# A chunked delta rule with an MLP on one core: K·Q^T and K·state as one product, and a new order of all steps

## The chip, the cores and the metric

The kernel runs on one core of one Trainium2 chip. The metric is the device time of one execution in microseconds (us). A core has a matrix engine (TensorE, PE in the profile, with its weight loads shown as PEld), a vector engine (VectorE, DVE), an activation engine (ScalarE, ACT), a general engine (GpSimd, POOL), and queues that start DMA transfers, most of them on SyncE (SP). Each engine works through its own instructions in order; engines wait for each other by semaphores. All data is 32-bit float.

## The reference

Two blocks stand one behind the other. The first is the delta rule, for 4 batches and 8 heads (32 heads), 768 tokens and 48 channels a head; the state of a head is a 48x48 matrix:

```python
k_n = k / (np.linalg.norm(k, axis=-1, keepdims=True) + 1e-06)
for t in range(S):
    y[:, :, t] = q_t @ state
    v_old = k_t @ state
    state = state + b_t * outer(k_t, v_t - v_old)
```

Its output, 384 channels a token, is x of the second block, an MLP with a residual:

```python
xn = (x - mu) / np.sqrt(var + 1e-06) * g_ln
out = x + np.maximum(xn @ w_ch1, 0.0) @ w_ch2      # 384 -> 1536 -> 384
```

## The kernel before, in words

The tokens are cut into 12 chunks of 64. The 32 heads lie in 16 columns of tiles, and in two halves of the 128 partitions; a product of one chunk for all heads is 64 small matmuls, four of them at a time in the four quadrants of TensorE's array. In the loop `for j ... for hp, e in hp_e`, `hp` picks the half of the partitions the operands are read from, and `e` the half that the result is written to.

Per chunk `c` the recurrence is written in matrices: G is K times K^T, from which VectorE computes a triangular inverse for the two halves of a chunk, row by row (`rows_inverse`, lines 910 and 917, for two chunks at once); `join` (lines 984 and 990) completes it with two small products. Then, in this order of dependence:

- `queries`: P = K times Q^T (line 822, into the PSUM tile `two`, 64 columns a head), and one VectorE instruction that multiplies it with a triangular mask into the tile `pt` (line 853). P does not need the state, so it may be made ahead.
- `recur`: `ks` = K times the state (line 1036 into `two`, 48 columns), which VectorE subtracts from v (line 1043); `qs` = Q times the state (line 1036 into `by`), which starts the sum of the output; `u` = inverse times v (line 1091 into `two`, copied to `u` by ScalarE, line 1093); `s` = K^T times u (line 1108), which VectorE adds to the state `s_all` (line 1118); `y` = P times u (line 1098), added to `qs` in `by` and copied to x by ScalarE (line 1136).
- LayerNorm of x (lines 1142 to 1154), a transposition, from chunk 3 on with a round trip through DRAM, and the MLP of that chunk. From chunk 3 on the first MLP product is computed with 15 block products per chunk (line 1311, sums on the other engines), the second with 7 (line 1527); chunks 1 and 2 use plain products for the first (line 1430), chunk 0 for both (lines 1410 and 1452).

Nothing but data links the MLP of one chunk with the recurrence of later chunks, so the steps of both are mixed. Every step (an engine, a function that issues its instructions, the keys that it reads and writes) is given to `Line.add`. The mixed order is written out by hand in the string `ORDER`: numbers of steps, and the letter `f` for a filler, a product of zeros with 256 columns (line 1605) that keeps TensorE busy. `emit` issues the steps in that order, and `in_this_order` pins the order on every engine, so a step that waits holds up all that stand behind it on its engine. The numbers in `cost`, `due` and `cap` belong to the planner that wrote the order and change nothing at run time.

`two` and `by` are two PSUM tiles of two banks each. G of later chunks, P, `ks`, `u` and `s` use `two`; `qs`, `y` and, from chunk 6 on, `join` use `by`. The MLP uses four other banks.

Of the kernel before, what the change touches and what calls it, by code (L numbers as in the profile page):

```python
# [16 lines left out]
C = 64  # L17
# [114 lines left out]
57 52 54 58-59 56 65-66 10-13 25 14 0 22 28 43 8 44 9 5 7 53 55 79 6 71 77 72 89 37 96 76 97 90 1-2 86 85 80 88 98  # L132
91 105 92 99 15 26-27 23 16 34-35 29-30 17 36 100 93 101 31 19 94 87 103 82 81 104 84 24 83 18 95 102 20-21 118 32
124 74 73 106-107 78 69 38 119 108 219-220 75 39 109 120 33 125 110-111 70 40 f 130-131 126 112 122 128 121 123 f f
f 132 134 400 113 405 64 63 262 257-258 313 411 256 260-261 263 404 410 259 311 68 322 312 403 310 399 324 323 325
67 409 402 408 398 133 136 135 41 45 62 254 225 129 127 231 137 f 140 145 213 138 211 235 139 144 142 141 f f f 146
143 241 245 f f 148 253 47 46 42 659 49-51 147 150 154-155 153 149 156 661 60-61 246 152 157 151 4 f f f 162-163 236
115 114 242 217 243 159 221 160 227 212 161 223 247 264 663 255 48 222 166-168 158 265-266 170-171 169 f f 164 f f
178 215 116 412 229 117 237 224 165 267-268 179 172 182 206-207 270 269 232 184 271-272 183 174 173 664 248 660 208
273 3 274-275 209 226 238 177 175-176 185 210 186-187 f f f 180 314 316 315 194 317 240 244 214 276 181 188 239  # L140
192-193 191 195 277-278 189 279 198 318-319 201 199-200 190 280-281 216 282 228 283 f 196-197 284 334 326 361 367
320 285-288 335 289-292 202 327 338 366 360 293-299 203-204 233 340 342-343 300 328-329 346 205 f f f f 330-331
347-348 671 218 397 230 396 234 352 336-337 339 353 332 354-355 572 574 673 665 662 341 251 249 573 344 575 358-359
250 345 349-350 576 578 406 362 577 579 301 407 321 333 432 431 309 307 302-303 308 304 473 306 305 471-472 474 788
351 356 363 357 252 658 415 433-434 582 580 598 370 364 581 599 373 435 604 583 605 368 584 610 586 365 413 470 414
611 585 588 416 372 587 475 590 401 787 790 792 789 791 793-794 589 379 417 591 378 592-596 616 600 374 597 602 601
606 418 376 603 608 436 666 369 476-479 481-489 480 490-495 375 496-499 670 675 672 1073 674 677 377 371 676 500
419-420 501 617 607 380 635 609 636 614 391 421 437 502-507 381 508 795 509 439 510-519 424 615 423 612 620 438 384
390 382 425 422 426 429-430 428 427 637 621 440-441 638 385 392 442 639 445 394 386 447 443 520-523 444 524 393
525-527 622-623 667 624 640 383 678 387 668 446 388 613 389 679-680 528 450 529 395 1085 625-626 618 530 451 448 455  # L150
531 456 449 452 532 650 533 457 534 453-454 535-536 651 537 641 627 642-643 628-629 644 796 458 462 645 630 538 652
539-544 653 631 464 460 465 619 646 461 463 459 826 921 1181 784 928 785 925 669 929 681 924 922 684 686 683 685 545
682 786 687 827 797 647 632 798-799 688-691 694 832 830-831 833 828 838 829 693 1087 1075 1077 1074 695-696 654
697-701 634 930 549 547-548 546 633 931-932 702-706 800 707-709 656 710 550 834 839 844-845 836 933 649 934-935 850
1079 1078 1089 1086 1076 853 851-852 466-467 837 551 859 842 835 552-555 1072 1084 556 860-861 840 862 557-558 560
559 711-713 655 714-715 692 716 561 717-728 562 801 863 841 846 802 864 805 854 856 866 927 843 857 855 936 729 565
564 563 566 865 803 807 806 730 810 808 848-849 809 811 815 812 847 731 804 876-877 869-870 732 813 871 937 567 872
814 733 816 734 817 735-736 822 818 886-887 878 820 825 568 823 819 570-571 569 821 824 468 867 858 469 1090 868 883
938-939 873 888-889 874 737 1080 738 941 890-891 940 942 1179 1176 1184 648 1178 1186 923 926 1177 1366 1188 1185
1187 1183 739-740 657 741 875 742-746 879 747-751 892 943 752-757 1365 1190 1189 880 894 881 895-896 944 901-902 897  # L160
903 898-899 946 945 1547 1088 1091 900 882 1092 1096 893 885 884 1081-1082 1191 975 1182 1558 1371 904 977 1093 905
947 978 1094 948 951 761 760 1083 1095 759 758 1097 1100 1373 1098-1099 983 912 906-907 913-915 984 989 916-917 1192
918 990 920 1370 1372 1375 1652 1377 1369 1376 1378 1180 1368 1379 1374 909 919 979 981 995 949-950 953-954 952 956
762 1193 763 1194-1195 982 765 996 980 985 1101 764 767 766 986 1559 972 908 910-911 1001 1004 969 1548 970 976 971
955 957 959 958 1102 1561 1549 1196 1103-1105 1107-1109 1002 1551 1550 1563 1110-1121 987 991 1010-1012 768 988 992
772 993 1003 1007 1122 1013-1015 769 994 770-771 999 1197 1000 1016 1020-1022 997 1027-1028 998 1198 1023-1024
773-775 777 1201 1199 1123 1560 1005-1006 1017 1008 1018 1565 1564 1553 1546 1552 1124-1125 960 974 1126-1135 1009
1019 1224 1034 1562 1136 1037-1040 1025 961 1654 1380 1137 1026 1200 973 1138 1029-1030 1035 1041-1042 1045
1031-1032 962-963 965 1367 964 1655 1658 1660 1662 1844 1664 1845 1139 1046 1381 1047-1048 1033 1043 1554 1049-1050
1052-1053 1225 1044 1228-1229 1226 968 967 778 966 1243 1232 1036 1051 1202 776 1203 1054-1055 1063 779 783 781-782  # L170
780 1056 1064-1065 1057 1066 1140 1382 1384 1383 1141 1204 1206 1142 1207 1205 1143 1058 1144 1244-1245 1233 1236
1234 1067 1237 1068 1239 1230 1247 1145 1385 1211 1235 1208 1146 1212 1147 1238 1209 1069 1248 1386-1387 1249
1240-1241 1227 1251 1266 1252 1059 1250 1242 1148-1149 1213 1210 1150 1214-1215 1388 1267 1231 1651 1070 1659 1846
1661 1275 1060 1246 1389 1216 1566 1151 1263-1264 1253 1256 1260-1261 1254 1262 1152-1153 1280 2047 1285 2035 1555
1257 1556 1271 1255 1154 1265 1268 1276 1269 1272 1155 1258 1156-1158 1270 1159 1273 1567 1277 1286 1281 1287
1160-1161 1259 1568 1278 1162-1164 1288 1165 1279 1289 1274 1166-1170 1062 1071 1657 1663 1219 1217 1220 1218 1557
1061 1222-1223 1221 1569 1650 1171 1573 1282 1390 1290 1303 1313 1291-1292 1314 1293 1304-1307 1315-1318 1308 1665
1309 1850 1574 1572 1571 1849 2141 1174-1175 1173 1653 1172 1294-1295 1297 1413 1296 1298 1301 1300 1299 1319
1283-1284 1666 1320 1310 1338 1330 1339 1420 1311 1302 2037 1312 1667 1106 1575 1321 1656 1327 1322-1323 1340
1331-1335 1341 1324-1325 1414-1415 1576-1577 1336 1345 1342-1343 1326 1417 1346 1328-1329 2036 1337 1570 1347 1418  # L180
1348-1350 1578-1579 1582 1351 1344 1679 1356 1391-1392 1424 1581 1352 1583-1584 1432 2039 1428 1456 2049 1421 1357
1416 1358-1361 1422 1429 1433 1585 1393 1586 1668 1587 1419 1588 1362 1589-1591 1395 1592-1593 1669 1430 1434
1425-1426 2038 1435 1353 1466 1447-1448 1461 2046 2051 1671 1423 1431 1670 1673 1672 1427 1594 1436 1444 1437 1445
1441-1442 1449 1595 1681 1596 1443 1450 1674 1452 1597 1396 1394 1451 1397 1400 1598-1599 1446 1600 1453 1462 1457
1438 1458 1676-1678 1675 1401 1454 1601 1455 1398 1602 1467-1468 1463 1603 1399 1604 1439 1605 1459 1606 1460 1680
1402 1607 1469 1682 1608 1494-1495 1484 1496 1471 1485 1472 1486-1487 1440 1470 1683 1488-1489 1684 1686 1475-1476
1478 1477 1490 1482 1403 1609-1610 1404 1473 1611 1464-1465 1474 2048 2040 1481 1479-1480 1852 1842-1843 1612 1860
1613 1501-1503 1497-1498 1504 1499 1354 1854 1851 1853 1855 1847 1364 1355 1363 2139 1856 2138 2143 1405 1857 1685
1492 1491 1483 1493 1858 1511 1505-1506 1614 1407 2145 1409 2146 2142 1408 1406 2148 2150 2147 2152 2149 1500 1512
1519 1615 1859 1616-1617 1513 1520 1514-1516 1618 1517 1521 2050 2041 1508 1518 1848 2034 1510 1522-1523 1526 1524  # L190
1527-1528 1525 1507 1529-1531 1688 1410 1687 1412 1709 1411 1619 1720 1509 1716 2052 1620 1689 1691 1532 1692
1696-1697 1690 1693 1621-1625 1698 2042 1694 1537 1871 1861 1713 1865 1862 1864 1863 1538 1710-1712 1539-1540 1714
# [1560 lines left out]
```

## Time and profile before

| what | value |
|---|---|
| three timed runs | 516.07, 517.01, 518.98 us (median 517.01) |
| profiled execution, first to last instruction | 514.1 us; no other time of it is given |
| TensorE busy | 493.1 us (96%) |
| VectorE busy | 353.5 us (69%) |
| GpSimd busy | 284.8 us (55%) |
| ScalarE busy | 206.9 us (40%) |
| P of chunk: line 822, `two`, from qt and kt, 64 matmuls in a chunk | 1.09 us in the chain |
| mask of P: line 853, 128x1024 | 1.22 us (median) |
| subtraction from v: line 1043, 128x768 | 0.94 us (median) |
| fillers: line 1605, 50 records | 13.8 us |

The profile shows one execution. Busy time of an engine is the time in which one of its compute instructions ran. The chain is followed back from the last instruction, at each step to what released it. A large matmul on the whole array leaves two records, a small one in a quadrant leaves one, so a group of 64 small matmuls is x64. A time in a list of groups can overlap the next group's by some tenths, since matmuls are pipelined; the chain's numbers do not overlap.

### The profile page before, as it was taken

The numbers are of one execution on the slowest core, as the hardware profiler recorded it, in microseconds if no ns is written. First come the engines' busy times: TensorE is split into PE (matmuls) and PEld (weight loads), VectorE is DVE, ScalarE is ACT, GpSimd is POOL, SyncE is SP. The second block draws the span as 40 slices with busy tenths as digits, with TensorE's granted clock in tenths as the row PEclk, the third lists the DMA queues.
The fourth block names the chain that finished last, engine by engine and source line by source line (L and its number), as shares of the span: only waits on it lengthen the run. The fifth ranks groups of instructions, "written<-read, shape, count | busy, mean of one in ns | idle before, by whom it ended". The sixth has DMA issues, their size and how long they took to land.

```text
span 514.1 us, 22905 instructions
## 1 busy us (share of the span) xinstructions
PE 493.1 (96%) x10022; PEld 450.7 (88%) x10022; DVE 353.5 (69%) x816; ACT 206.9 (40%) x462; POOL 284.8 (55%) x447
## 2 busy tenths in 40 slices
PE   5897899999999999999999999999999999999997
PEld 3675797668888898999999999999999999999996
DVE  4688479899994999975997847898727346254241
ACT  4785764422533333351434343423514425324140
POOL 2634583144658879749477465283274551844644
PEclk9999999999999999999999999999999999999999
DMA  8958895577338755387454474313660321202011
GB/s 207 251 83 192 221 191 127 128 173 117 67 60 207 123 117 92 73 221 123 80 108 62 105 203 76 99 15 53 132 149 12 88 36 41 57 13 82 8 24 31
DMA packets 181635, 54.56 MB, mean 106 GB/s; under 512 B 164888, under 2 KB 177312, under 8 KB 181536
## 3 DMA queue, kind: packets, MB, share of 16 engines
q1 hardware_dynamic: 168512, 40.10, 37.4%
q10 hardware_dynamic: 10816, 9.83, 6.3%
q0 software_dynamic: 2208, 3.17, 4.3%
q8 instruction: 78, 1.28, 1.1%
q14 instruction: 21, 0.17, 0.1%
HBM read 36.30 MB, written 16.78 MB: 103 GB/s over the span
## 4 chain that ended last, share of the span: by engine, by line
PE 85%; DVE 5%; DMA 3%; issue 2%; ACT 1%; SPq 1%; POOL 1%; DVEq 0%; ACTq 0%; POOLq 0%
PE f L1527 28%; PE f L1311 24%; PE f L1430 6%; PE two L822 3%; PE f L1452 3%; DMA tb<-in_q_dram 2%; PE by L1098 2%; PE by L1036 2%; PE two L1091 2%; PE two L1036 2%; PE two L1108 2%; PE f L1605 1%; DVE xb L917 1%; SPq L404 1%; DMA kr<-in_k_dram 1%
## 5 line engine op out<-in xcount | busy, mean ns | idle before, releaser
L1527 PE MATMUL f<-w_sb,h_all 128*128 128x192 f32 x396 | 83.9, 330 | 0.0
L1514 POOL TENSOR_TENSOR h_all<-h_all 128x256 f32<-128x256 f32 x99 | 74.8, 767 | 9.4 <-PE f L1527 3.3
L1527 PE MATMUL f<-words,h_all 128*128 128x192 f32 x396 | 79.5, 329 | 0.2 <-POOL h_all L1514 0.2
L1552 POOL TENSOR_TENSOR words<-h_all 128x128 f32<-128x128 f32 x66 | 30.2, 478 | 74.4 <-ACT h_all L1338 50.2
L1334 DVE TENSOR_TENSOR h_all<-f,h_all 128x512 f32<-128x512 f32 x72 | 49.2, 686 | 30.5 <-PE f L1311 25.9
L1527 PEld LDWEIGHTS f<-w_sb,h_all 128*128 128x128 f32 x396 | 65.3, 190 | 1.6 <-POOL h_all L1514 0.2
L1527 PEld LDWEIGHTS f<-words,h_all 128*128 128x128 f32 x396 | 65.1, 190 | 1.6 <-POOL h_all L1514 1.0
L910 DVE TENSOR_TENSOR tmp<-xb,gb 128x31 f32<-128x31 f32 (+19 forms) x139 | 56.0, 403 | 3.7 <-POOL xb L897 0.5
L917 DVE TENSOR_TENSOR xb<-xb,tmp 128x31 f32<-128x31 f32 (+19 forms) x139 | 51.4, 370 | 2.5
L1329 ACT COPY h_all<-f 128x512 f32<-128x512 f32 x45 | 25.8, 586 | 62.9 <-PE f L1311 39.3
L404 POOL DMA_DIRECT2D tb<-in_k_dram x64 | 41.9, 658 | 8.2 <-PE f L631 7.1
L1338 ACT ACTIVATE h_all<-h_all 128x512 f32<-128x512 f32 x54 | 32.5, 626 | 30.0 <-DVE h_all L1334 29.8
L1311 PE MATMUL f<-x_new,w_sb 128*128 128x128 f32 x288 | 41.4, 278 | 0.0
L1311 PE MATMUL f<-xnt,w_sb 128*128 128x128 f32 x288 | 40.4, 278 | 0.1
L1311 PEld LDWEIGHTS f<-x_new,w_sb 128*128 128x128 f32 x288 | 37.4, 191 | 0.4
L1311 PEld LDWEIGHTS f<-xnt,w_sb 128*128 128x128 f32 x288 | 36.8, 191 | 0.5 <-issue 0.2
L1430 PE MATMUL f<-xnt,w_sb 128*128 128x256 f32 x144 | 33.9, 383 | 0.0
L1430 PEld LDWEIGHTS f<-xnt,w_sb 128*128 128x128 f32 x144 | 26.7, 190 | 3.5
L605 POOL TENSOR_TENSOR w_sb<-words 128x768 uint32<-128x768 uint32 (+1 forms) x11 | 15.3, 1400 | 23.7 <-issue 18.2
L1545 DVE TENSOR_TENSOR o<-f,x 128x192 f32<-128x192 f32 x33 | 11.2, 348 | 24.9 <-PE f L1527 17.2
L1136 ACT COPY x<-by 128x384 f32<-128x384 f32 x23 | 10.6, 481 | 42.6 <-DVE o L1545 27.2
L1527 PE MATMUL f<-w_sb,words 128*128 128x192 f32 x132 | 27.6, 332 | 0.0
(247 smaller groups left out, 1003.6 us busy)
## 6 DMA issues: line engine op xcount, KB each, us to landing
words<-in_moe_w_ch_dram ACTq DMA_DIRECT2D x20, 384.0 KB, 5.2
gd<-gsb SPq DMA_DIRECT2D x11, 512.0 KB, 4.1
v<-in_v_dram SPq DMA_DIRECT2D x24, 192.0 KB, 3.6
kr<-in_k_dram SPq DMA_DIRECT2D x46, 96.0 KB, 3.7
out_dram<-o SPq DMA_DIRECT2D x46, 96.0 KB, 2.5
xld<-xlt SPq DMA_DIRECT2D x9, 384.0 KB, 3.6
xnt<-xld SPq DMA_DIRECT2D x36, 96.0 KB, 3.0
tb<-in_q_dram SPq DMA_DIRECT2D x40, 64.0 KB, 3.5
```

The source lines that it names most:

```text
L404: add(eng, cost, lambda: QUEUE[eng].dma_start(out=out_, in_=in_), r, w, bulk=n * ns / 16e3, np=n, **kw)
L910: lambda j=j, n=n, w=w, t=t: nc.vector.tensor_tensor(out=t, in0=xv[:, 0:n, j : j + 1].to_broadcast([128, n, w]), in1=gv[:, j : j + 1, j + ...
L917: "DVE", dve(n * w), lambda t=t, rest=rest: nc.vector.tensor_tensor(out=rest, in0=rest, in1=t, op=ALU.subtract),
L1036: nc.tensor.matmul(dst[half(e), hp, j], src[drows(hp), (e if n else key_half(c, hp, e)) * GP + j], s_all[drows(hp), e, j], start=(n == 0 o ...
L1311: nc.tensor.matmul(wide(p[:, f : f + 128]), w[:, f : f + 128], r, start=start and i == 0, stop=True, skip_group_check=True)
L1329: add("ACT", act(512), lambda: nc.scalar.copy(o, p), pk, ok)
L1334: add("DVE", dve(512), lambda: nc.vector.tensor_tensor(out=o, in0=x, in1=y, op=op), [*xk_, *yk], ok)
L1338: add("ACT", act(512), lambda: nc.scalar.activation(o, o, ACTF.Relu, scale=scale), [], ok)
L1430: nc.tensor.matmul(p[:, 0:TOK], w1_sb[:, t, f * 128 : (f + 1) * 128], xnt[:, t], start=(t == 0), stop=(t == KC - 1))
L1514: add(eng, cost, lambda: e.tensor_tensor(out=out_, in0=x, in1=y, op=op), r, w, port=2 if eng == "Pool" else 1, pr=-2)
L1527: lambda f=f, t=start and f == order[0]: nc.tensor.matmul(p[:, 0:D2], lhs(f), rhs[:, f], start=t, stop=(f == order[-1]), skip_group_check=True
L1552: lambda f=f + i: e.tensor_tensor(out=s3[f], in0=one(0, 0)[0](f), in1=one(1, 0)[0](f), op=ALU.subtract),
```

## The change

From the fourth chunk on (`c >= JOINT`, 3), P and `ks` are one product. Its moving operand is a tile `qs_all` that holds, head by head, 64 columns of Q^T and 48 of the state next to each other, so `qts[0]` and `s_all` become views of it. The stationary operand, K, is loaded once per head and half instead of twice. The result has 112 columns a head, four heads in a bank; the heads with `hp` 0 go to `two`, those with `hp` 1 to `by`. `queries` is not called for these chunks.

In the old P the heads with `hp` 1 were written to the exchanged half of the partitions; the joint product can't do that, since the state's part must stay. So the mask is now three VectorE instructions of 512 elements: two on 64 partitions that exchange the halves, and one on 128. The subtraction from v is two instructions of 384. `qs` follows as before, but behind the instructions that read `by`.

The string `ORDER` is new from its first word to its last, for all engines, chunks 0 to 2 included. It has 47 fillers where the old one has 25; in both all of them stand ahead of the first MLP product. The work of all other steps is the same.

```diff
@@ ORDER = ... (all of it)
...
+    JOINT = 3
...
-    qts = [sb(f"qt{i}", [128, GH, C]) for i in range(NQT)]
+    qs_all = sb("qs", [128, GH, C + D])
+    qts = [qs_all[:, :, 0:C], sb("qt1", [128, GH, C])]
...
-    s_all = sb("s_all", [128, 2, GP, D])
+    s_all = qs_all[:, :, C:].rearrange("p (e j) d -> p e j d", e=2)
...
-        if c:
-            def state(dst, src, n):
...
+        def state(dst, src, n):
...
+        if 0 < c < JOINT:
             pe(64, lambda: state(p_2, kt, 0), ktk + ["s_all"], TWO, 0.65, name=f"ks{c}", **kp_e)
             pe(64, lambda: state(p_y, qt, 1), qtk + ["s_all"], [*BY, "qs"], 0.65, name=f"qs{c}", **kp_e)
             v_j = vv.rearrange("p (j n) d -> p n j d", n=2)
             add("DVE", dve(768), lambda: nc.vector.tensor_tensor(out=v_j, in0=v_j, in1=p_2, op=ALU.subtract), TWO, vk, **kw)
+        if c >= JOINT:
+            W, B2 = C + D, GP // 2
+
+            def keys_by():
+                for j in range(GP):
+                    for hp, e in hp_e:
+                        o = j % B2 * W
+                        nc.tensor.matmul(
+                            (two, by)[hp][half(e), j // B2, o : o + W], kt[drows(hp), key_half(c, hp, e) * GP + j],
+                            qs_all[drows(hp), e * GP + j],
+                        )
+            add("PE", 1.6, keys_by, ktk + qtk + ["s_all"], [*TWO, *BY], np=64, arr=1.2, name=f"PK{c}", **kp_e)
+            both = [t[:, :, 0 : B2 * W].rearrange("p b (j x) -> p b j x", x=W) for t in (two, by)]
+            v_b = vv.rearrange("p (b j n) d -> p n b j d", b=2, n=2)
+            p_b = pt.rearrange("p (b j n) t -> p n b j t", b=2, n=2)
+            for hp in (1, 0):
+                add(
+                    "DVE", dve(384),
+                    lambda hp=hp: nc.vector.tensor_tensor(out=v_b[:, hp], in0=v_b[:, hp], in1=both[hp][:, :, :, C:], op=ALU.subtract),
+                    (TWO, BY)[hp], vk, **kw,
+                )
+            for hp, pi, po in ((1, half(0), half(1)), (1, half(1), half(0)), (0, slice(0, 128), slice(0, 128))):
+                n = pi.stop - pi.start
+                add(
+                    "DVE", dve(512),
+                    lambda hp=hp, pi=pi, po=po, n=n: nc.vector.tensor_tensor(
+                        out=p_b[po, hp], in0=both[hp][pi, :, :, 0:C],
+                        in1=pmask[pi, None, None, :].to_broadcast([n, 2, B2, C]), op=ALU.mult,
+                    ),
+                    [*(TWO, BY)[hp], "pmask"], [("pt", one_of(c))], **kw,
+                )
+            pe(64, lambda: state(p_y, qt, 1), qtk + ["s_all"], [*BY, "qs"], 0.65, name=f"qs{c}", **kp_e)
...
-        queries(c, pr=pr - 1, lag=0.5)
+        if c < JOINT:
+            queries(c, pr=pr - 1, lag=0.5)
```

More of the change, by code (lines that the diff above doesn't have):

```diff
@@ L137 @@
[L137 to L171, printed above, removed]
@@ L248 @@
+2986 3028-3029 3010-3011 2989 2991-2992 3002 3001 2974 3012-3013 3030-3033 3020-3027 3018 3014-3015 3035-3038 3016
+3034 3039 3017 3019 3040 3046 3041 3047-3049 3043 3042 3050-3052 3044 3053 3045 3054
 """
```

202 lines of the change are left out of this document (115 added, 87 removed).

## The prediction

> **What bounds the kernel now.** I read the page first (engines, slices, chain), then busy time by stretches of 20 us, the chain in order of time, and the timeline of TensorE and VectorE for the first 145 us.
>
> ```profile
> span 514.1 us, 22905 instructions
> ...
> PE 493.1 (96%) x10022; PEld 450.7 (88%) x10022; DVE 353.5 (69%) x816; ACT 206.9 (40%) x462; POOL 284.8 (55%) x447
> ...
> PE   5897899999999999999999999999999999999997
> ...
> PEclk9999999999999999999999999999999999999999
> ...
> PE 85%; DVE 5%; DMA 3%; issue 2%; ACT 1%; SPq 1%; POOL 1%; DVEq 0%; ACTq 0%; POOLq 0%
> ```
>
> TensorE carries 85% of the chain at full clock. Its gaps lie in the first five slices.
>
> ```profile
> 0.00:20.00 20.00, 13.91 (x263) 8.99 (x264) 11.35 (x51) 11.36 (x24) 6.46 (x17) 1.00 0.93 260
> 20.00:40.00 20.00, 17.29 (x468) 13.29 (x471) 14.06 (x39) 16.11 (x40) 10.95 (x20) 1.00 0.65 96
> 180.00:200.00 20.00, 20.00 (x438) 18.25 (x427) 19.31 (x38) 6.46 (x16) 16.66 (x24) 1.00 0.60 118
> 200.00:220.00 20.00, 19.59 (x492) 18.34 (x491) 19.00 (x38) 7.07 (x16) 16.22 (x22) 1.00 0.34 70
> ```
>
> The columns are stretch, length, then busy us of TensorE, its weight loads, VectorE, ScalarE and GpSimd. TensorE idles 6.1 and 2.7 us in the first two stretches; from 120 to 500 us it idles 1.2 us in all. So two regimes: a front up to the first MLP product (58.0 us), set by the chain of the first inverse, and behind it a stretch where each microsecond of TensorE work is a microsecond of time. VectorE is 96% busy between 180 and 220 us, without holding TensorE up.
>
> The products in question, from the chain in order of time (start, length, what, records):
>
> ```profile
> 339.47 1.09 PE two L822 x64
> ...
> 352.66 1.08 PE two L1036 x64
> ...
> 365.07 1.08 PE by L1036 x64
> 366.15 0.93 PE two L1091 x64
> ...
> 372.31 0.86 PE two L1108 x64
> ...
> 456.84 11.61 PE f L1311 x104
> ```
>
> L822 is P (K times Q^T, 64 columns a head), L1036 into `two` is K times the state (48 columns), into `by` Q times the state. 64 and 48 moving columns cost the same 1.09 and 1.08 us; with 48 stationary columns (L1108) the same count takes 0.86. So the small products go by their stationary side or a fixed pace, 17 ns apiece, four quadrants in turn, not by moving columns. L1311 is the MLP, 112 ns per record of 128 columns.
>
> **The joint product.** From chunk 3 on, nine chunks, P (1.09) and K·S (1.08) leave: 2.17 us. One product of 64 matmuls with 112 columns enters, which no row shows. Lower end: still bound by the stationary side, 1.09. Upper end: strictly by columns from P's pace, 1.09 × 112/64 = 1.91. Between: L1311 gives 0.87 ns per column and record (112/128), and the 42 records of L1430 with 256 columns last 9.26 us in the chain, 220 ns each, hence 0.85 per added column. 112 columns are 95 ns; 64 matmuls over four quadrants are 16 rounds, 1.52. A group that follows another small one takes 0.93 (L1091), one behind an MLP record 1.08, so entering costs up to 0.15; I take half, 1.60. Both ends lie far off; this one rests on the moving rows, where 112 columns belong. Saved: 2.17 − 1.60 = 0.57, times 9 = 5.1 us, all of it on the bounding engine (ends 2.3 and 9.7).
>
> The Trainium skill, "TensorEngine Tiling (Array Packing)", Instruction Overhead, says that a matmul of one column takes as long as one of about 60, and so charges by columns only above that. The equal 48- and 64-column rows agree with it; by it alone 112 columns would sit near the upper end, and the saving would be 2.3 us rather than 5.1.
>
> **VectorE.** Out per chunk: the mask of P in one instruction (128x1024, 1.22) and the subtraction from v (128x768, 0.94), 2.16. In: two subtractions of 384 elements, priced by L1077 (128x384, 0.56), and three masks of 512, priced by L853's shape of 128x512 in the front (0.67); two of those run on 64 partitions only, but nothing shows that this shortens them. 1.12 + 2.01 = 3.13, so +0.97 a chunk, 8.7 us over the run. They are also later: P no longer waits for the state's update only in the old K·S; now P's mask stands in the serial part. Q·S (into `by`) must wait for both half masks and the subtraction that read `by`; U stands behind it in TensorE's queue; ScalarE's copy of U, the state's update and the next joint product wait for U. Cover by the new order: MLP work of 2.60 us between joint product and Q·S in chunks 3 and 10, 3.1 to 10.3 us in the others. What must be done in that time in chunk 10 is 0.67 + 0.56 + 0.56 + 0.67 = 2.46 plus a semaphore; in chunk 3, 1.90 behind tail steps of an inverse. So it just fits; I charge 0.5 us for the whole run. Ends: 0, and 8.7 if no cover works.
>
> The joint product also needs both banks `two` and `by`, so the join of the two half inverses, which uses `by` from chunk 6 on, must now be copied out before it. In the order, the state's update has 10 to 36 us of TensorE work before the next joint product from chunk 3 on (old: 11 to 28), ample for 0.95 us of state addition. Last chunk: 60.0 us of MLP stand behind the last Y (old 55.6), so the final LayerNorm and its DRAM round trip are covered and the end of the run keeps its shape.
>
> **The new order of the front.** The work before the first MLP product is unchanged, but 47 zero products (L1605) stand there instead of 25. One is 0.52 us (six records in 1.57), so 22 more are 11.5 us. Idle to fill: 6.1 + 2.7 us, and 4.0 us in the waits between 40 and 58 us, 12.8 in all, 4.4 of it at the very start. There the new order puts the two iotas on GpSimd ahead of its two beta DMAs (1.21 us), and VectorE's zeros third; the first TensorE work can start some 2 us sooner. The identity, though, is now behind one more GpSimd copy, a memset and a DMA issue (0.61, 0.96, 0.65), about 1 us later than its 5.8. Added up by hand along the new queues with the durations of before: the first product of level 1 of the inverse comes at 17.5 (old 16.1, but its two halves now directly behind each other; the old second half came at 18.3), level 2 at 25.1 (23.4), held by fillers, level 3 at 31.6 (29.1), level 4 at 36.5 (34.4), level 5 at 43.1 (41.4). The old order then lost 1.56 us at 43.8 in a wait with no releaser in the profile; I do not charge it again, and reach the first MLP product at 59.0 (58.0). I take +1.0. Ends: −1 (that wait gone, fillers free) and +11.5 (all fillers on top).
>
> SyncE's loads are reordered as well: one load of chunk 3's keys now precedes chunk 2's q blocks (0.45 us of issue). The chain had those q blocks (4.9 us at 72.7), hidden under the 30 us of MLP work that TensorE has by then; nothing charged; uncovered, it costs 0.45. VectorE has 2 us more in front of the end of the second inverse; TensorE comes to that point 1.3 us of work plus the front's 1.0 later, so up to 0.7 may show; it is inside the 0.5 and the range.
>
> **Sum.** −5.1 + 1.0 + 0.5 = −3.6: span 514.1 to 510.5. The page gives no other time of that execution; the three timed runs (516.07, 517.01, 518.98) are 2.0 to 4.9 us longer than its span, so I apply the difference to their median: 513.4 us.
>
> **Rivals.**
> 1. The front pays for its fillers. For: TensorE's waits there are short (0.2 to 0.8 us apart from the start and one of 1.56), so fillers have few holes to sink into, and my walk has them holding level 2. Against: the chain has ScalarE and VectorE steps between products that no filler delays. All on top: −5.1 + 0.5 + 11.5 = +6.9, 523.9 us. It turns the sign when the first MLP product starts after 58.0 + 4.6 = 62.6, and is slower beyond noise after 65.2.
> 2. The joint product goes by columns, 1.91: −2.3 + 1.0 + 0.5 = −0.8, 516.2 us. For: above some count columns must set the pace. Against: the 0.85 ns of the MLP's records.
> 3. VectorE becomes the bound: 19.3 of 20 us busy at 180 leaves no room for 0.97 more a chunk; Q·S waits each time: −5.1 + 1.0 + 8.7 = +4.6, 521.6. Against: in 160 to 180 VectorE is busy 14.6 of 20 us, so its queue runs ahead in between.
> The Trainium skill says the same in "TensorEngine Tiling (Array Packing)", PSUM Bottleneck: tiling speeds TensorE, and emptying PSUM may become the limit. No run here shows it yet; the idle of 1.2 us speaks against it so far.
> 4. The joint product stays bound by its stationary side (1.09) and the front gains 0.5: −9.7 − 0.5 + 0.5 = −9.7, 507.3.
>
> **How the numbers follow.** 0.5% (2.6 us) is about what a measurement of this kernel can tell from no change. Forecast 0.47 (its own range 511 to 515.5, of which 0.05 lies within 0.5%), rival 1 0.20, rival 2 (with half-paid fillers, which land there too) 0.17, rival 3 0.06, rival 4 0.10. Faster: 0.42 + 0.10 = 0.52. Slower: nearly all of 1 and 3, 0.25. Same: 0.05 + 0.17 and the rest, 0.23. The range 508.5 to 521.5 leaves out the far half of rivals 4 and 1.
>
> **What would show it.** The joint product's group: about 1.6 us for 64 records; 1.9 means rival 2. First MLP record at 59 ± 2 us; past 63 means rival 1. TensorE idle between 120 and 500 us of 1 to 2 us; above 5, with VectorE as releaser in front of Q·S or U, means rival 3. Filler records 94 instead of 50. VectorE busy about 362 us. I am wrong if the front moves by more than 4 us or TensorE stops being filled behind it.

## The result, and the profile after

The changed kernel takes 523.11 us (median of 20 runs, 517.27 to 527.51), the kernel before 517.03 (20 runs, 515.74 to 519.76). The ratio is 1.0095, 95% interval 1.0072 to 1.0117: about 1% slower. Ratios leave out the runs that lie over 1.5% above the fastest of their kernel: of the changed kernel's 20 that is three, and the other 17 have a median of 522.55. The forecast was 513.4 us, the range 508.5 to 521.5. The profiled execution of the changed kernel took 519.89 us with a span of 518.2; the one of before had 514.1.

The same lines of the page as were shown of before (span, engines, slices of TensorE and of its clock, chain):

```profile
span 518.2 us, 21844 instructions
...
PE 502.9 (97%) x9490; PEld 457.6 (88%) x9490; DVE 364.8 (70%) x843; ACT 208.3 (40%) x462; POOL 282.0 (54%) x447
...
PE   8998898999999999799999999999999999999997
...
PEclk9999998999999999999999999999999999999999
...
PE 88%; DVE 7%; ACT 3%; issue 1%; POOL 0%; POOLq 0%; DVEq 0%; ACTq 0%
```

TensorE has become busier (97% for 96%), which here is no good sign: 22 more zero products are in that number. Two digits matter: the 7 in slice 17 of TensorE, where all slices around it are 9, and the 8 in slice 7 of its clock, where before had 9 throughout. The stretches of 20 us (stretch, length, busy us of TensorE, its weight loads, VectorE, ScalarE and GpSimd, then granted clock, DMA share, GB/s):

```profile
0.00:20.00 20.00, 17.84 (x282) 12.15 (x286) 11.93 (x49) 11.71 (x25) 6.66 (x17) 1.00 0.84 215
20.00:40.00 20.00, 19.72 (x511) 16.04 (x502) 13.35 (x39) 14.75 (x34) 10.97 (x17) 1.00 0.86 162
...
80.00:100.00 20.00, 18.60 (x436) 15.35 (x437) 16.30 (x33) 9.95 (x22) 5.63 (x6) 0.83 0.41 101
...
200.00:220.00 20.00, 16.81 (x407) 15.79 (x406) 18.84 (x35) 7.52 (x18) 14.63 (x21) 1.00 0.29 59
```

From 200 to 220 us TensorE idles 3.2 us (0.4 before). From 80 to 100 us the clock is 0.83 in the mean. The waits of TensorE (line, releaser, us in total, times, longest) name both places:

```profile
PE by L1032 <- DVE pt L1066: 2.9, 1, 2.9
PE f L1634 <- DVE u L420: 1.5, 1, 1.5
PE f L981 <- issue: 1.4, 1, 1.4
```

L1032 into `by` is Q times the state, here of chunk 5, waiting for the masks (L1066). L981 is the join of chunk 1's half inverses, 64 products of 32 by 32; "issue" means that the profile shows nothing it waited for. Finer stretches show what follows that wait:

```profile
84.00:86.00 2.00, 0.60 (x64) 0.49 (x50) 2.00 (x3) 0.00 (x0) 1.10 (x1) 1.00 0.49 164
86.00:88.00 2.00, 2.00 (x25) 1.73 (x29) 1.86 (x6) 0.68 (x3) 1.66 (x3) 0.55 0.50 39
88.00:90.00 2.00, 2.00 (x62) 1.91 (x56) 1.83 (x5) 1.93 (x5) 0.27 (x1) 0.50 0.69 214
90.00:92.00 2.00, 2.00 (x12) 2.00 (x10) 1.90 (x5) 0.25 (x1) 0.00 (x0) 0.50 0.97 218
```

TensorE idles 1.4 of 2 us, and from the next stretch on its clock is 0.5 for 6.83 us in the trace's record of the clock: up to 3.4 us of work lost behind a wait of 1.4.

**How each run divides.** Every run lists its mean granted clock, so span times (1 − clock) is the work that the run lost to half clock if TensorE was the bound in all of it. Medians (the kernel before: 78 of the 80 runs beside the experiments; changed: the 17 runs):

| kernel | us | lost to the clock | rest |
|---|---|---|---|
| before | 517.3 | 2.1 | 514.7 |
| changed | 522.6 | 6.8 | 516.3 |

Counted so, 4.7 of some 5 us are clock. That is the most it can be: from run to run the time rises by only 0.6 us for each us so counted, in both kernels. So the clock makes some 3 to 5 of the 5 us, and a "rest" is too low where much clock was lost. Of the changed kernel's 20 runs, the two with a clock of 0.995 took 517.27 and 517.94 us; those at 0.984 or below 521.6 to 527.5. The profiled execution lost 3.4 and stands 3 us below the median.

**Where the profiled execution's 4.1 us come from.** I add up, line by line, the time from each matmul's start to the next one's start, from the first MLP product (58.02 us before, 60.84 after) to 520 us. The lines of P, of K and Q times the state and of the joint product take 22.31 + 24.51 = 46.82 us before and 10.91 + 14.31 + 15.50 = 40.72 after: −6.1. The joint product is not worth all of that. A joint product takes 1.69 us (median of the nine groups), P 1.09 and K times the state 1.08, so 0.48 are saved in a chunk and 4.3 in the run. The old lines also hold 2.3 us of waits without a releaser, which did not come again, and the new ones 0.9 of half clock.

Against the −6.1: first MLP product 2.8 us later, chunk 5's wait +2.9, the wait at L981 +1.4, half clock +2.5 (3.4 less the 0.9 that the lines hold already). That is +3.5; the other 0.6 are not assigned.

The joint product itself (group, us in total, mean ns | idle before it), and VectorE's groups around it:

```profile
L1048 PE MATMUL two<-qs,kt 48*64 48x112 f32 x288 | 16.1, 259 | 0.0
L1048 PE MATMUL by<-qs,kt 48*64 48x112 f32 x288 | 15.8, 259 | 0.0
...
L1066 DVE TENSOR_TENSOR pt<-by,pmask 64x512 f32<-64x512 f32 x18 | 12.4, 689 | 5.8 <-PE by L1048 3.3 <-ACT h_all L1367 1.6 <-ACT xnt L1209 0.5
...
L914 DVE TENSOR_TENSOR xb<-xb,tmp 128x256 f32<-128x256 f32 x4 | 6.4, 1593 | 0.1
...
L914 DVE TENSOR_TENSOR xb<-xb,tmp 128x255 f32<-128x255 f32 x8 | 4.1, 507 | 0.2
```

Nine products at 15.50 us are 1.72 each in the mean. The last two groups are the clue to chunk 5: four instructions of one shape average 1593 ns, where those of nearly the same size take 507. VectorE's timeline (start, us, line, operation) has the one that did it:

```profile
202.44 4.41 DVE L914 TENSOR_TENSOR xb<-xb,tmp 128x256 f32<-128x256 f32 x1
206.77 0.17 DVE L1172 BATCH_NORM_AGGREGATE mv<-st 128x2 f32<-128x6 f32 x1
206.86 0.52 DVE L1171 BATCH_NORM_STATS2 st<-x 128x6 f32<-128x384 f32 x1
207.42 0.18 DVE L1172 BATCH_NORM_AGGREGATE mv<-st 128x2 f32<-128x6 f32 x1
207.63 0.68 DVE L1066 TENSOR_TENSOR pt<-by,pmask 64x512 f32<-64x512 f32 x1
```

and GpSimd's, over the same time:

```profile
202.45 2.48 POOL L1300 TENSOR_TENSOR w_sb<-w_sb 128x512 f32<-128x512 f32 x2
204.90 0.45 POOL L1323 TENSOR_TENSOR ident<-xnt 128x128 f32<-128x128 f32 x1
205.31 1.25 POOL L1300 TENSOR_TENSOR w_sb<-w_sb 128x512 f32<-128x512 f32 x1
```

GpSimd ran without a break until 206.56, and VectorE's update of the inverse ended just behind that, at 206.85. The joint product was done near 203.8; its first mask began at 207.63. The Trainium skill, "SBUF — State Buffer", SBUF: two separate sides, says that VectorE, with two operands in SBUF, and GpSimd take turns at one port as a lock held for a whole instruction; the trace agrees that VectorE is shut out, 4.41 us here against 0.41 for the same instruction in the second experiment below. But here it stayed out over four GpSimd instructions in a row, not over one.

The kernel before has such rows as well, and the prediction did not price them:

```profile
183.78 0.36 DVE L917 TENSOR_TENSOR xb<-xb,tmp 128x192 f32<-128x192 f32 x1
184.17 2.44 DVE L910 TENSOR_TENSOR tmp<-xb,gb 128x207 f32<-128x207 f32 x1
```

There, too, GpSimd worked without a break, from 184.14 to 187.20 us, but nothing came of it: TensorE was busy 20.00 of the 20 us from 180 on.

### The profile page after: what moved, and what is told of

Read it like the earlier page. It is cut to its first block, busy times and chain, and to the rows that moved or that the text cites. A ratio compares the mean times of both kernels' runs of the same rounds, so it can differ in the third digit from the quotient of the medians.

```text
span 518.2 us, 21844 instructions
## 1 busy us (share of the span) xinstructions
PE 502.9 (97%) x9490; PEld 457.6 (88%) x9490; DVE 364.8 (70%) x843; ACT 208.3 (40%) x462; POOL 282.0 (54%) x447
## 4 chain that ended last, share of the span: by engine, by line
PE 88%; DVE 7%; ACT 3%; issue 1%; POOL 0%; POOLq 0%; DVEq 0%; ACTq 0%
PE f L1556 29%; PE f L1340 21%; PE f L1459 6%; PE f L1439 4%; PE f L1481 3%; PE f L1634 2%; PE by L1032 2%; PE by L1127 2%; PE two L819 2%; PE two L1048 2%; PE two L1137 2%; DVE xb L914 2%; PE two L1120 2%; DVE tmp L907 1%; PE f L617 1%
## 5 line engine op out<-in xcount | busy, mean ns | idle before, releaser
L1543 POOL TENSOR_TENSOR h_all<-h_all 128x256 f32<-128x256 f32 x99 | 72.1, 743 | 19.5 <-PE f L1556 7.9
L1556 PE MATMUL f<-w_sb,h_all 128*128 128x192 f32 x396 | 81.2, 330 | 0.0
L1556 PE MATMUL f<-words,h_all 128*128 128x192 f32 x396 | 76.9, 331 | 0.0
L914 DVE TENSOR_TENSOR xb<-xb,tmp 128x31 f32<-128x31 f32 (+19 forms) x139 | 56.7, 408 | 3.0
L907 DVE TENSOR_TENSOR tmp<-xb,gb 128x31 f32<-128x31 f32 (+19 forms) x139 | 53.0, 381 | 3.9
L1340 PE MATMUL f<-x_new,w_sb 128*128 128x128 f32 x288 | 39.8, 276 | 0.0
L1634 PE MATMUL f<-u 128*128 128x256 f32 x94 | 25.3, 402 | 2.7 <-DVE u L420 1.5
L1556 PE MATMUL f<-w_sb,words 128*128 128x192 f32 x132 | 26.0, 332 | 0.0
```

The costliest lines, as they stand in the source:

```text
L907: lambda j=j, n=n, w=w, t=t: nc.vector.tensor_tensor(out=t, in0=xv[:, 0:n, j : j + 1].to_broadcast([128, n, w]), in1=gv[:, j : j + 1, j + ...
L914: "DVE", dve(n * w), lambda t=t, rest=rest: nc.vector.tensor_tensor(out=rest, in0=rest, in1=t, op=ALU.subtract),
L1340: nc.tensor.matmul(wide(p[:, f : f + 128]), w[:, f : f + 128], r, start=start and i == 0, stop=True, skip_group_check=True)
L1543: add(eng, cost, lambda: e.tensor_tensor(out=out_, in0=x, in1=y, op=op), r, w, port=2 if eng == "Pool" else 1, pr=-2)
L1556: lambda f=f, t=start and f == order[0]: nc.tensor.matmul(p[:, 0:D2], lhs(f), rhs[:, f], start=t, stop=(f == order[-1]), skip_group_check=True
L1634: nc.tensor.matmul(f_[0][:, 256:512], nought, nought[:, 0:1].to_broadcast([128, 256]))
```

## Experiments

Theory A: the joint product gains, and the new order loses more. Theory B: the joint product is what loses. Theory C: the 22 additional zero products are. A2 and A3 are A, sharpened by what the runs before had shown. Steps are told by their numbers in the written order; an `f` is a zero product.

**1. Front alone, fillers alone, joint product alone, order alone.**

`front_old`: all steps ahead of the first joint product in the old order, the rest in the new.

```diff
 ORDER = """
-52 54 56-57 59 58 10-11 5 12 7 13 15 14 25 66 65 43 17 0 34 29 35 26 28 47 41 8 254 60 9 45-46 55 53 6 39
+57 52 54 58-59 56 65-66 10-13 25 14 0 22 28 43 8 44 9 5 7 53 55 79 6 71 77 72 89 37 96 76 97 90 1-2 86 85 80
...
```

> The changed kernel with every step ahead of chunk 3's joint product back in the order of the kernel before, its 25 zero products among them; from the joint product on the new order. Theory A (the joint product gains about 0.44 us nine times, 4 us in all, and the new order loses more: 2.8 us in the front, clock at half speed for some microseconds, 2.9 us in chunk 5): the first MLP product back at 58 us, 3 us won or, if the front also brings the loss of clock, 6 to 8; 515 to 520.5 us, still a wait of 2 to 3 us in chunk 5. Theory B (the joint product itself loses about 1 us a chunk, VectorE and a longer serial chain): the front's 2.8 us come back and no more, 519.5 to 521 us, with TensorE's waits in several chunks. Theory C (the 22 additional zero products alone): about 516 us, as before, nothing left to find behind the front.

Measured: 522.75 us (518.51 to 524.84), ratio 1.0113 (1.0072 to 1.0154). A miss: no gain. The profile has the first MLP product at 61.15, behind a wait of 2.3 us without a releaser at 55 us, and the wait in chunk 5 with half clock behind it:

```profile
204.00:208.00 4.00, 3.44 (x86) 3.21 (x82) 3.93 (x5) 0.85 (x3) 2.80 (x3) 1.00 0.01 4
208.00:212.00 4.00, 1.64 (x61) 1.64 (x64) 3.89 (x9) 1.47 (x5) 2.98 (x5) 0.79 0.15 32
212.00:216.00 4.00, 4.00 (x85) 3.91 (x81) 3.90 (x12) 0.80 (x1) 0.00 (x0) 0.50 0.21 42
```

Its runs lost 7.0 us to the clock. So chunk 5's wait costs up to 6.3 us rather than 2.9. The run does not clear the front: the wait at 55 us stands between the same two matmuls in the kernel before and in `front_old_c5` below, where it lasts 0.65 and 0.56 us. So it put back the first MLP product of this one execution.

`fill25`: 22 zero products left out, nothing else.

```diff
 ORDER = """
...
-108 73 104 f 109-110 23 100-101 211 78 40 111 f f f f f 84 95 102
+108 73 104 f 109-110 23 100-101 211 78 40 111 f 84 95 102
...
```

> The changed kernel with 22 of its 47 zero products left out (the last ones of the longest rows); all else in the new order. Theory A (the new order as a whole): the first MLP product at 60 us or later still, the total within 2 us of the changed kernel, 520 to 524 us. Theory C (the zero products themselves cost the front its 2.8 us): first MLP product at 58 us, 3 us or more faster, 517 to 520 us. If the zero products keep the clock up, the granted clock in the first 100 us gets lower and the time longer, above 524 us.

Measured: 521.98 us, ratio 1.0091 (1.0056 to 1.0126). The first MLP product comes at 62.6, later than with 47, and the front of this profile has 10.24 us of half clock (5.1 us lost). Theory C falls: without the 22 the kernel is no faster. That they keep the clock up is not shown: its runs lost 7.3 us to the clock, the changed kernel's 6.8.

`joint_old`: the joint product in the old order, and `order_new`: the two old products in the new order.

```diff
 ORDER = """
...
-1056-1060 1142 1209 1385 1210-1211 776 779 782-783 1215 1388 1386-1387 1389-1390 1065-1068
+1066-1067 1059 1068 1142 1385 1143 1208 1210 1144 1211 1209 1145 1060 1146 1248-1249 1237
...
```

```diff
 ORDER = """
-57 52 54 58-59 56 65-66 10-13 25 14 0 22 28 43 8 44 9 5 7 53 55 79 6 71 77 72 89 37 96 76 97 90 1-2 86 85 80 88 98
+52 54 56-57 59 58 10-11 5 12 7 13 15 14 25 66 65 43 17 0 34 29 35 26 28 47 41 8 254 60 9 45-46 55 53 6 39
...
+1140 1205 1381 1206-1207 776 779 782-783 1211 1382-1383 1385 1063-1066 1236 1067
...
```

> The joint product, its masks and subtractions put into the order of the kernel before: the joint product where K times the state stood, Q times the state just ahead of U with at least 2.9 us of MLP behind the joint product, the front and its 25 zero products as before. Theory A: the joint product's gain is left without the loss of the new order, 517.0 less 4, 512 to 515 us, clock above 0.99. Theory B: the joint product is what loses, 519 to 524 us, TensorE waits on VectorE ahead of Q times the state in most chunks.

> The code of the kernel before (P and K times the state as two products) in the new order: both stand, one behind the other, where the joint product stands, the mask and the subtraction at their places there. Theory A: all that the new order loses without the gain of the joint product, 523 plus 4, 525 to 528 us, first MLP product at 61 us. Theory B: without the joint product the new order does no harm, 514 to 518 us.

Measured: 559.63 and 540.70 us (ratios 1.084 and 1.048). Both miss by far, and neither tells what it was made for, since each got waits of its own. In `joint_old` the MLP waits for VectorE and GpSimd in nine places; in `order_new` K times the state had to wait seven times for the mask of P, which sits in the same bank:

```profile
PE f L1351 <- DVE h_all L1374: 8.8, 5, 4.0
PE f L1567 <- POOL h_all L1554: 6.7, 4, 3.7
```

```profile
PE two L1037 <- DVE pt L854: 12.2, 7, 3.1
```

`order_new2`, with P (1381 in chunk 5) and its mask (1382) at least 3 us of TensorE work ahead of K times the state (1383), came out no better, and stays inconclusive too (547.43 us, ratio 1.0578; the largest of its waits are 4.1 us of an MLP product for VectorE, and 3.4 us of a product in the front and 3.3 us of a join for ScalarE):

```diff
-1140 1205 1381 1206-1207 776 779 782-783 1211 1382-1383 1385 1063-1066 1236 1067
+1381-1382 1554 1051 1203 778 777 775 1204 1054-1058 1140 1205-1207 776 779 782-783 1211 1063-1066 1383 1385 1236 1067
...
```

> The code of the kernel before in the new order, P at least 3 us of TensorE work ahead of K times the state, so that its mask is done by then (in the earlier kernel of this kind it was not, 12.2 us of waits). Theory A2: the changed kernel plus 9 times 0.44 less the wait in chunk 5 that its masks bring, and its loss of clock: 521 to 527 us, clock below 0.99. Theory B (the joint product at fault): 514 to 518 us.

A hand-made order of the whole run can't be compared within 1%. From here on single steps were moved.

**2. Chunk 5's wait.** `c5fix` moves VectorE's update of the inverse (step 1142) and three LayerNorm steps behind the masks:

```diff
-1142 1209 1385 1210-1211 776 779 782-783 1215 1388 1386-1387 1389-1390 1065-1068
+1385 776 779 782-783 1388 1386-1387 1389-1390 1209-1211 1215 1065-1068
...
-1143 1392
+1142-1143 1392
```

> The changed kernel with four VectorE steps (one update of the inverse, 128x256, that took 4.41 us while GpSimd worked without a break, and three small steps of a LayerNorm) moved from the place ahead of chunk 5's masks to the place behind them. Theory A2 (a wait of 2.9 us ahead of chunk 5's Q times the state, and clock at half speed behind it): the wait is gone, TensorE's idle in 200 to 220 us falls from 3.2 to below 0.5, the clock lost there as well, 517 to 520.5 us. If the front and the stretch at 84 us carry the loss instead, 520.5 to 523 us. Theory B (the joint product itself): 523 us, the wait comes up at another VectorE step.

Measured: 519.73 us (513.18 to 521.79, 12 runs), ratio 1.0015 (0.9981 to 1.0049) after 1.0095: 0.8%, some 4 us, won by moving four small instructions, and clear of the noise. The update now finds GpSimd idle:

```profile
205.36 0.41 DVE L921 TENSOR_TENSOR xb<-xb,tmp 128x256 f32<-128x256 f32 x1
```

The lost clock falls from 6.8 to 4.1, the rest from 516.3 to 513.5 (medians of 17 and 9 runs). Its profile still has the wait of 1.4 us at 84 us, this time with no half clock behind it. Instead of 2.9 us for the masks, TensorE now waits 1.3 us at U, for ScalarE's copies of the inverse, which stand behind the LayerNorm's steps.

`warm` leaves the wait and puts five products of zeros into it (adding zeros to an accumulator):

```diff
+    def warm():
+        nc.tensor.matmul(f_[1][:, 256:512], kraws[2][:, 0:128], pad.to_broadcast([128, 256]), start=False, stop=True, skip_group_check=True)
...
+w w w w w
 1391 1143 1392
```

> The changed kernel with five products of zeros, 2.7 us, put into TensorE's queue right ahead of chunk 5's Q times the state, where it waits 2.9 us. No wait is shortened: they only keep TensorE at work in it. Theory A2 (the granted clock follows how busy TensorE was in the 3.41 us before): no half clock behind 207 us, 1.7 to 3.4 us less lost in the runs that had it, 520 to 522 us, mean granted clock up by 0.003 to 0.006. Rival (the loss of clock comes from elsewhere): same clock and same time as the changed kernel, 523 us, or up to 0.5 more for the products.

Measured: 521.84 us (520.14 to 523.43, 6 runs), ratio 1.0075 (1.0046 to 1.0105). This run does not decide: its interval overlaps the changed kernel's, and its mean granted clock, 0.9885, is the changed kernel's 0.9884, where 0.003 to 0.006 more was forecast. No half clock stands behind 207 us in its profile, but none does in the changed kernel's profile either. Other waits of the run bring half clock, one of them in the front (behind ScalarE's copies):

```profile
PE by L783 <- ACT xt L741: 2.8, 1, 2.8
```

**3. The small products at 84 us.** `c5_e1` is `c5fix` with chunk 1's first join (421), Q times the state (438) and second join (426) each set back by one or two MLP products:

```diff
-375 437 421 504 439 1077 377 678 1087 1076 608 384 425 385 609 601 422 424 390 423 380 438 606 614 426 615
+375 437 504 439 1077 377 678 1087 1076 608 384-385 609 601 390 380 606 421 425 422 424 423 614 438 615
...
-622-623
+426 430 428 427 429 622-623
```

> As the kernel with the four VectorE steps moved, and in chunk 1 the products of 32 by 32 behind K times the state (L981) stand two MLP products later, with Q times the state and the second join set back likewise, so that fewer small products follow each other at 78 to 85 us, where TensorE waited 1.4 us for nothing that the profile names. Theory A2: that wait below 0.7 us, no half clock at 86 us, 515 to 518 us. If that wait is not due to the row of small products: as the kernel with the four steps alone, 517 to 520.5 us.

Measured: 517.29 us (515.17 to 519.83, 12 runs), ratio 0.9990 (0.9963 to 1.0017), lost clock 3.6. The wait without a releaser is 0.3 us instead of 1.4, and the stretch is full:

```profile
80.00:100.00 20.00, 19.13 (x566) 14.59 (x565) 18.77 (x37) 11.65 (x24) 7.06 (x8) 1.00 0.38 98
```

In time, `c5_e1` cannot be told from `c5fix` (the intervals overlap), and 517.29 lies in both ranges of the expectation; what it shows is the wait in the trace. With these steps moved, the loss of 1% is gone.

The row of small products alone does not make such a wait: in the changed kernel 120 or more matmuls start within 2 us at 18 places, and only here TensorE then idles over 0.4 us. The traces have a better sign. In the 17 profiles, 51 of the 57 waits without a releaser of over 0.5 us (from 5 us on) end 1.2 to 1.7 us after a packet of 16 KB has landed in a DMA queue of kind "instruction" (here: landed at 84.43, TensorE goes on at 85.92). Of the 106 such waits with a named releaser 3 do, and of times drawn at random 7%. So in these waits TensorE most likely lacked instructions. No run changed that, and why the packet came late at this place is open.

**4. The price of the joint product.** `joint_twice` is `c5_e1` with each joint product issued twice; `two_twice` is the kernel before with P and K times the state issued twice in the same nine chunks. Neither changes a result.

```diff
-            add("PE", 1.6, keys_by, ktk + qtk + ["s_all"], [*TWO, *BY], np=64, arr=1.2, name=f"PK{c}", **kp_e)
+            add("PE", 1.6, lambda: (keys_by(), keys_by()), ktk + qtk + ["s_all"], [*TWO, *BY], np=64, arr=1.2, name=f"PK{c}", **kp_e)
```

```diff
-            pe(64, lambda: prod(range(2)), keys, [*pk, *w], 0.86, name=f"{'GP'[n]}{c}", **kw)
+            pe(64, lambda: [prod(range(2)) for _ in range(2 if n and c > 2 else 1)], keys, [*pk, *w], 0.86, name=f"{'GP'[n]}{c}", **kw)
...
-            pe(64, lambda: state(p_2, kt, 0), ktk + ["s_all"], TWO, 0.65, name=f"ks{c}", **kp_e)
+            pe(64, lambda: [state(p_2, kt, 0) for _ in range(2 if c > 2 else 1)], ktk + ["s_all"], TWO, 0.65, name=f"ks{c}", **kp_e)
```

> The kernel with the steps of chunks 5 and 1 moved (517.3 us), and each of the nine joint products issued twice, with the same result. It measures the price of a joint product where it stands: 9 times 1.52 to 1.73 us if TensorE is the bound there, 531 to 533 us. By the prediction's two ends: 9 times 1.09 gives 527, 9 times 1.91 gives 534.5. If joint products stand beside waits, less than 527.

> The kernel before with P and K times the state issued twice in chunks 3 to 11, with the same result. Theory A: 9 times 1.9 to 2.17 us more than 517.2, 534 to 537 us, so 3 to 5 us more than the doubling of the joint product adds. Theory B (the two products are no dearer than the joint one): within 1.5 us of what the doubling of the joint product adds.

Measured: 532.40 us, as forecast, and 542.10, a miss: 5 us above its range, with 6.5 us of lost clock. By time the joint product costs (532.40 − 517.29) / 9 = 1.68 us, the pair (542.10 − 517.4) / 9 = 2.74, or, without the lost clock, (531.1 − 514.5) / 9 = 1.84 and (536.1 − 514.7) / 9 = 2.38. By the lines in the traces (58 us on), a second joint product takes (29.88 − 15.51) / 9 = 1.60 us, a second pair 2.08, leaving out 3.4 us more waits without a releaser. The saving is 0.48 to 0.54 us a chunk, 4.3 to 4.9 us in the run. Theory B falls.

**5. Where the rest of the saving goes.** `c5_e1` only draws level with the kernel before. `pool_v` moves GpSimd's sum of an expert's weights (238) ahead of the scaling of v (214) in the changed kernel's front; `best` has that, the moves of `c5_e1`, and ScalarE's copies 780 and 781 ahead of the LayerNorm:

```diff
-214 253 187 186 227 367 185 237 663 238 f f
+187 186 227 367 185 237-238 214 253 663 f f
...
-776 779 782-783 1388 1386-1387 1389-1390 1209-1211 1215 1065-1068 1240 1069 1248 1212 968 1236 781 780 1213
+776 779 782-783 780-781 1388 1386-1387 1389-1390 1209-1211 1215 1065-1068 1240 1069 1248 1212 968 1236 1213
```

> The changed kernel with the one move on GpSimd in the front: its sum of an expert's weights ahead of the scaling of v, which waits for a load until 43.7 us. Theory A2: ScalarE's wait at 43 us gone, first MLP product 0.5 to 2 us sooner than 60.5, and the half clock that some runs have behind 49 us: 520 to 522.5 us. If the loss of the front lies elsewhere: 523 us, first MLP product at 60.5.

> The kernel with the four VectorE steps of chunk 5 and the small products of chunk 1 moved, and two more moves of steps against waits that its trace shows: two ScalarE copies of an inverse go ahead of a LayerNorm's two steps in chunk 5 (U waits 1.3 us for them), and GpSimd's sum of an expert's weights (L602) goes ahead of the scaling of v in the front (ScalarE waits 4.7 us for it at 43 us with three copies of the first inverse behind it, TensorE 0.2 to 2.8 us). Theory A2 (what the new order loses are these waits and the clock behind them; the joint product's gain is there): 513 to 515.5 us, 0.4 to 0.8% faster than before. If the joint product gains nothing: 516.5 to 518.

Measured: `pool_v` 522.67 us, ratio 1.0089 (1.0057 to 1.0120); `best` 517.24, ratio 0.9995 (0.9968 to 1.0022). Both miss, and `best` lands where its expectation has no gain of the joint product; the doubling speaks against that reading. ScalarE's copies do come 3.8 us sooner in `pool_v` (45.23 for 49.07), but TensorE then waits 1.7 us at the same product (L778) without a releaser, the first MLP product comes at 61.30, and chunk 5's wait is still there:

```profile
PE by L1039 <- DVE pt L1073: 2.9, 1, 2.9
PE by L778 <- issue: 1.7, 1, 1.7
```

and `best` trades the 1.3 us at U for other waits:

```profile
PE f L1446 <- ACT h_all L1454: 2.2, 3, 1.3
...
PE f L1347 <- POOL x_new L1330: 1.7, 1, 1.7
```

`front_old_c5` joins the old front with chunk 5's moves, `front_old_c5a` adds ScalarE's copies, and `front_new` is the mirror: the kernel before with the new front.

```diff
 ORDER = """
-52 54 56-57 59 58 10-11 5 12 7 13 15 14 25 66 65 43 17 0 34 29 35 26 28 47 41 8 254 60 9 45-46 55 53 6 39
+57 52 54 58-59 56 65-66 10-13 25 14 0 22 28 43 8 44 9 5 7 53 55 79 6 71 77 72 89 37 96 76 97 90 1-2 86 85 80
...
-1142 1209 1385 1210-1211 776 779 782-783 1215 1388 1386-1387 1389-1390 1065-1068
+1385 776 779 782-783 1388 1386-1387 1389-1390 1209-1211 1215 1065-1068
...
```

> Both at once: every step ahead of chunk 3's joint product in the order of the kernel before with its 25 zero products, and behind it the new order with the four VectorE steps of chunk 5 moved. Alone, the old front gave 522.8 us (with a wait of 2.9 and 3.4 us of lost clock in chunk 5, and a wait of 2.3 for nothing named at 55 us), the four steps 519.7. Theory A3 (the joint product saves 4 to 5 us of TensorE work and the new front gives them away: by 60 us it has done 5 us less of useful TensorE work): 512 to 515.5 us, faster than before by 0.4 to 1%. Rival (the order of the front does not matter, the gain is lost elsewhere): 517 to 520 us.

> The same with two ScalarE copies of an inverse in chunk 5 ahead of a LayerNorm's two steps (U waits 1.3 us for them in the kernel with the four steps moved). Theory A3: 511 to 515.5 us; the wait of 1.3 us may come back at an MLP product that then waits for GpSimd, as it did with the new front, and then it is as fast as without. Rival: 516 to 520 us.

> The other way round: the code of the kernel before, with every step ahead of chunk 3 in the new order and its 47 zero products, from there on its own order (K times the state and what follows it in chunk 3 set back by 2 to 3 us of MLP work, since the new front has done some of that already). Theory A3: the front's loss alone, 3 to 5 us more than before, with lost clock 519 to 524 us, and by 60 us 25 to 27 us of useful TensorE work done where the kernel before has 30. Rival: 516 to 518.5 us.

Measured: 516.11 us (ratio 0.9991, 0.9965 to 1.0017), 515.61 (0.9989, 0.9961 to 1.0017), and 530.23 (1.0263). All three miss their ranges under theory A3, the second by 0.1 us. The first two are the fastest medians of all, and still not to be told from before (516.76 beside them). Their first MLP product is back at 58.4, and their rest is 513.5 to 513.7, one us under `c5_e1` and under the kernel before. So the front's order is worth some 1 us in the end, within the noise, and not the 4 that were looked for. The mirror has waits of its own (3.4 us at an MLP product at 73 us) and tells nothing.

Where the last 3 to 4 us of the saving go shows in part. In the profile of `front_old_c5` the lines of P, K and Q times the state and the joint product take 12.40 + 15.54 + 16.12 = 44.06 us, 3.3 more than in the changed kernel for the same products. Of that, 1.3 are the wait at U, which follows Q times the state, and 1.7 are waits without a releaser at four places. `front_old_c5a` is without the wait at U, and has 1.7 us at an MLP product that waits for GpSimd in its place. The remainder is open.

## Why the prediction was wrong

- **Joint product: right.** Forecast 1.60 us a piece and 5.1 us saved; measured 1.69 in the typical group against 1.09 and 1.08, hence 4.3, and 4.3 to 4.9 by the doubling. Rivals 2 and 4 are out: 1.69 lies well between 1.09 and 1.91, and against 16 rounds of 95 ns the entry is 0.17 instead of 0.08. That the lines fell by 6.1 in the profile is in part luck: 2.3 of it are waits of the old execution.
- **Front: mis-sized.** +1.0 forecast, first MLP product 2.8 us later. It is within the ends. The order of the steps does it: the old front has its first MLP product at 58.0 to 58.6 us in five of six profiles (61.15 in `front_old`), the new one with its 47 zero products at 59.1 to 64.5 in ten. Rival 1 blamed the 22 zero products, and without them the front was no faster, so that its 523.9 us lies close to the measured time by chance.
- **Stalls: the sum of 0.5 us failed.** The cover of 2.60 us between the joint product and Q times the state was held against 2.46 us of VectorE work, instruction by instruction, as if VectorE were free when the joint product ended. In chunk 5 the cover was 3.4 us, but VectorE stood in a 4.41 us update and three LayerNorm steps until 207.6, and the wait was 2.9. Rival 3 named the place (Q times the state behind the masks) but not this cause, and priced it over all chunks; it happened in one.
- **The term that was missing: the clock.** "TensorE carries 85% of the chain at full clock" was read as a property of the kernel. It was one of that execution. It lost under 1 us to the clock (mean 0.999), where the median run of that kernel loses 2.1 and of the changed one 6.8. Each wait was priced at its own length, where a wait of 1.4 us cost up to 3.4 more. This step makes some 3 to 5 of the 5 us.
- **Signs to watch for.** VectorE's busy time was forecast as 362 us and is 364.8, filler records 94 as forecast; idle from 120 to 500 us is 3.7 us, between the 2 and 5 that were set as bounds, all but 0.5 of it between 200 and 220 us. The first MLP product lies within its 59 ± 2. So none of the signs set for being wrong came up: none of them watched the clock.
- **Sum.** −6.1 + 2.8 + 2.9 + 1.4 + 2.5 + 0.6 = +4.1 in the profiled execution, for −3.6 forecast; the median execution loses another 3 us or so to the clock.

## What to carry to other kernels

Where TensorE is busy nearly throughout, price a wait of over a microsecond at its length plus the half clock that may follow, and look at the mean granted clock of every run, not of one profile. In front of a short serial chain on VectorE, look at what GpSimd does at that moment: a small instruction there can last as long as GpSimd's row of work. A saving measured at the instruction is not yet a saving of time: nine products became 4 to 5 us cheaper, and after all repairs the run can't be told from the one before.

## What was not expected of the hardware

The stretches of half clock are 3.41, 6.83 or 10.24 us long in the records, and within a profile all changes lie on one grid of 3.41 us, so the clock is set anew at that step. Laying that grid over 17 profiled executions (the ends of each left out) and taking TensorE's busy share in each window at full clock gives how often the next window was at half clock:

| TensorE busy in the window | windows | next at half clock |
|---|---|---|
| under 0.45 | 13 | 13 |
| 0.45 to 0.55 | 23 | 15 |
| 0.55 to 0.65 | 20 | 6 |
| 0.65 to 0.75 | 45 | 1 |
| over 0.75 | 2392 | 0 |

So 1.5 to 1.9 us of idle in one window were enough in 15 of 23 cases, more always, 1.2 to 1.5 in 6 of 20. Where a wait lies on the grid, which differs from run to run, decides: in the changed kernel's profile the 2.9 us of chunk 5 fell into two windows (0.45 and 0.69) and cost no clock, in `front_old` into one (0.17), with two windows of half clock behind it. The Trainium skill, "TensorE: Matmul & The Clock Gate", What's actually happening, has the free-running window of 3413 ns, which the records agree with, starting at another point in each run; its rule in HAM oscillation, that gaps over about 3.4 us are to be avoided, is too mild for this kernel.
